# Forgetting attention and a bilinear FFN on one core: row sums of P on the tensor engine in batches 0 and 1, in a new order of work

## The chip, the cores and the metric

The program runs on one core of a Trainium2 chip. The core has a matrix engine (TensorE, here PE, with its weight loads shown apart as PEld), a vector engine (VectorE, DVE), a scalar engine (ScalarE, ACT), a general engine (GpSimd, POOL) and a queue engine (SyncE, SP) that here only issues DMAs. Data lie in SBUF, 128 partitions wide; PE writes to PSUM, eight banks of 128 x 512 fp32. The metric is the device time of one execution in microseconds. The kernel before takes 419.19 us (median of two runs, 418.51 and 419.87).

## The reference

Two stages. First attention with a forget gate, for 8 batches, 8 heads, 576 positions and a head size of 64:

```
scores = q @ k^T / 8
cum    = cumsum(log(clip(f, 1e-4, 1)))          # over positions
scores = scores + cum[query] - cum[key], and -1e9 above the diagonal
P      = exp(scores - rowmax);  P = P / sum(P)
x      = P @ v
```

Then, with x laid out as 4608 tokens of 512 numbers, `out = ((x @ w_a) * (x @ w_b)) @ w_out` with an inner width of 1536.

The term cum[query] is the same for a whole row of scores, so the softmax drops it; the kernel needs only cum[key].

## The kernel before, in words

**Tiles.** A tile t is a pair of heads of one batch: 8 batches x 4 pairs = 32 tiles, numbered 4 x batch + pair. The 576 query rows of a tile fall into blocks i = 0 to 3 of 128 rows and block 4 of 64 rows. For the blocks 0 to 3 both heads have their own rows of scores; for block 4 the two heads lie in the upper and lower 64 partitions. Scores are grouped in PSUM tiles `sc` (two buffers): group 0 holds blocks 1 and 0, then 2, 3 and 4.

**A tile's stages.** q and k are loaded (`load_qk`, from SP), cast to fp16 (`cast_qk`), transposed on PE into PSUM `psT` and copied to `qT` and `kT`. PE makes the scores (line 390). For batch 0 PE adds the decay to them, from the row `crow`, which holds cum as a high and a low fp16 part, and DVE takes the row maxima (line 474). For the other batches DVE adds the decay from `spread`, a copy of cum on all partitions, and takes the maximum in the same instruction (line 500). ACT makes P = exp (lines 527 and 531) into `PA` (blocks 0 to 2) or `PB` (blocks 3 and 4), in fp16, and with `accum_out` the row sums too, which come out by one more ACT instruction, the accumulator read. DVE takes their reciprocals (lines 539 and 541), POOL multiplies P by them (line 549). Then P is transposed: for batch 0 on PE through PSUM `psP` (line 569) and a copy, for the others by a DMA issued on SP (line 563). PE multiplies with v (`do_pv`, line 591; `do_pv4` for block 4, line 607) into the bank `pv`, which has one buffer, and DVE casts the result into x, stored transposed as `xT` (lines 217 and 618). For the batches 0 and 1 this is done in two parts, blocks 0 and 1 and blocks 2 and 3, so that the first tokens are ready early.

**FFN.** `ffn` takes 256 to 512 tokens at a time: 12 times `psa` and `psb` on PE (line 861), ACT's cast of psa to `a`, DVE's product `ht` (line 872); then `pso` (line 881), a copy to `osb` and a store. It needs the x of all four tiles of its tokens, and the weights, which POOL loads with a cast (line 365). `psa`, `psb`, `pso`, `psT`, `psP` and `scd` share three PSUM banks, `ff`.

**Start.** f is loaded four times in quarters of 32 partitions (two DMAs from ACT's queue, two from POOL's, line 173), clipped, passed through ln, summed by a scan on DVE (line 187), and made into `crow` (lines 189 and 190). SP stores cum to DRAM, from where `spread` is read.

**Order.** Every piece of work is an `Op` with its engine or engines, a planned duration, dependencies and a priority. A planner has used them once; what the program runs is its answer, written out in two strings. `ORDER` is the sequence of all ops, and `CHOICE` the engine of each op that could go to several (D, A or P). Each engine runs its instructions in this sequence. Dependencies and durations of an `Op` no longer act when the program is built; waits come from the data that the instructions read and write.

Of the kernel before, what the change touches and what calls it, by code (L numbers as in the profile page):

```python
# [9 lines left out]
FP32 = mybir.dt.float32  # L10
# [15 lines left out]
def kernel(  # L26
# [39 lines left out]
    lowrow = perm.tile([128, 1], FP32, tag="lowrow", name="lowrow")  # L66
# [3 lines left out]
    def constants():  # L70
        make_identity(nc, ident16)
        nc.gpsimd.memset(lowrow, 0.0)
        for x in pickh:
            nc.gpsimd.memset(x, 0.0)
        for m in range(4):
            x = slice(32 * m, 32 * m + 32)
            nc.gpsimd.tensor_copy(out=pick[x, :], in_=ident16[x, x])
            nc.gpsimd.tensor_copy(out=pickh[m // 2][x, :], in_=ident16[x, x])
            if m % 2:
                nc.gpsimd.memset(lowrow[x, :], -1.0)  # L80
# [12 lines left out]
    def paddings():  # L93
        for x in PB:
            nc.gpsimd.memset(x[:, 12, 64:128], 0.0)
        for i in range(2):
            nc.gpsimd.memset(nv[i][64:128, NSB - 1, :, :], 0.0)
# [11 lines left out]
            "LA0": 1, "LA1": 1, "LA2": 1, "LA3": 1, "PA": 4, "PB": 2, "PTA": 3, "PTB": 2, "st": 6, "ht": 14, "a16": 3, "osb": 2,  # L109
# [13 lines left out]
    osb_pool = pool("osb", RING["osb"])  # L123
    ps = pool("ps", 1, space=bass.MemoryType.PSUM)
# [35 lines left out]
    def f_tiles():  # L160
        x = [s_pool.tile([128, 1024], FP32, tag="S", name=n) for n in ("cum_f", "cum_l")]
        cw["f"], cw["l"] = (t[:, 0:S] for t in x)
        cw["1"], cw["h"] = (t[:, S:].bitcast(FP16)[:, 0:S] for t in x)

    def f_load(_):
        f_rows(nc.scalar, 0)

    def f_rows(eng, c):
        if not cw:
            f_tiles()  # L170
# [7 lines left out]
    o_f = Op("ACT", 2.05, f_load, prio=-310, land=0.3)  # L178
    s_users = [take(o_f, "S") for _ in range(2)]
    o_f2 = Op("POOL", 1.3, lambda _: f_rows(nc.gpsimd, 1), prio=-310, land=0.3)  # L180
    o_c = Op("POOL", 4.5, lambda _: constants(), prio=-300)
    o0 = Op("DVE", 0.3, lambda _: (nc.vector.memset(warm, 1.0), nc.vector.memset(cw["1"], 1.0)), prio=-300)
    o_w = Op("ACT", 2.2, warm_table(LN), [o0], prio=-300)
    o1 = Op("DVE", 0.45, lambda _: nc.vector.tensor_scalar(out=cw["f"], in0=cw["f"], scalar1=1e-4,
                                                           scalar2=1.0, op0=MAX, op1=MIN), [o_f, o_f2], prio=-300)
    o2 = Op("ACT", 0.7, lambda _: nc.scalar.activation(out=cw["l"], in_=cw["f"], func=LN), [o1, o_w], prio=-300)
    o3 = Op("DVE", 1.35, lambda _: nc.vector.tensor_tensor_scan(
        out=cw["f"], data0=cw["1"], data1=cw["l"], initial=0.0, op0=MUL, op1=SUB), [o2, o0], prio=-300)
    o4 = Op("DVE", 0.45, lambda _: nc.vector.tensor_copy(out=cw["h"], in_=cw["f"]), [o3], prio=-300)
    o5 = Op("DVE", 0.75, lambda _: nc.vector.scalar_tensor_tensor(  # L190
        out=crow, in0=cw["h"], scalar=lowrow[:, 0:1], in1=cw["f"], op0=MUL, op1=ADD), [o4, o_c], prio=-300)
# [4 lines left out]

    o6 = Op("SP", 1.1, cum_store, [o3], prio=-300, land=0.4)
    o_e = Op("ACT", 1.4, warm_table(EXP), [o2], prio=-300)
    for u in s_users:
        u.extend([o_f2, o0, o1, o2, o3, o4, o5, o6])  # L200
# [79 lines left out]
    PSPREAD = {t for t in range(4, 8)}  # L280
    DECP = tuple(range(1))
# [240 lines left out]
    def do_exp(t, i, h):  # L522
# [3 lines left out]
        if i == 4:  # L526
            nc.scalar.activation(out=p_blocks(t, 4), in_=T[("s" if direct else "z", t, 4)], func=EXP, bias=st[:, 8:9],  # L527
                                 scale=sign, accum_out=st[:, 18:19])
# [49 lines left out]
    def do_pv(t, rows, parts):  # L578
# [6 lines left out]
        for j in range(rows[-1] + 1):  # L585
            for i in rows:
# [7 lines left out]
                first = False  # L594

    def do_pv4(t, o=None):
# [5 lines left out]
        if own:  # L602
            o = ps.tile([128, 512], FP32, tag="pv", bufs=1, name="pv4")[:, 0:64]
        T[("pv4", t)] = o
        for j in range(NSB):
# [9 lines left out]

    def do_ev4(t):
# [5 lines left out]
    EXPD = {0: 0.39, 1: 0.505, 2: 0.61, 3: 0.72, 4: 0.775}  # L622
    NORM = {0: 0.37, 1: 0.48, 2: 0.6, 3: 0.7, 4: 0.74}
# [14 lines left out]
    def attention(t, base):  # L638
# [12 lines left out]
        if not direct:  # L651
            if t in PSPREAD:
# [3 lines left out]
                for h in range(2):  # L656
                    bm = Op("PE", 512 * COLS, lambda _, h=h: spread_mm(t, h), [o5, bc0] + bcs, prio=prio(0) - 5, mode="full", name=f"bm{t}")
# [15 lines left out]
        for gs in ([(0,), (1,), (2, 3)] if b in EARLY else [(0, 1), (2, 3)]):  # L673
            deps = [kq_ops[(w, b, pr)] for w in "qk"] + [o_c] + ([o5] if direct else bcs)
# [27 lines left out]
            for u in (kq_users[("q", b)], kq_users[("k", b)]):  # L702
                u.append(qk)
        for g, gi in [(g, groups[g]) for g in ((0, 1, 3, 2) if t in MASKP else (0, 1, 2, 3))]:
            qk, sc, su = qk_of[g], sc_of[g], None
            for i in gi:
                part = part_of(t, i)
                mxs = []
                for h in range(1 if direct else 2):
# [22 lines left out]
                    mxs.append(mx)  # L732
                es = []
                for h in range(1 if i == 4 else 2):
                    ex = Op("ACT", EXPD[i], lambda _, i=i, h=h: do_exp(t, i, h),
                            mxs if i == 4 or direct else mxs[h:h + 1], prio=prio(g),
                            name=f"exp{t}.{i}")
                    ex.tail = 0.005
# [15 lines left out]
                su.extend(es)  # L754
                rc = Op("DVE", 0.16, lambda _, i=i: do_recip(t, i), es, prio=prio(g))
# [75 lines left out]
        for rows in ([(0, 1), (2, 3)] if b in EARLY else [(0, 1, 2, 3)]):  # L831
# [3 lines left out]
            pv = Op("PE", n * 128 * COLS * 1.05, lambda _, rows=rows, parts=parts: do_pv(t, rows, parts),  # L835
# [3 lines left out]
            ev = Op("DVE", 0.15 + 0.00106 * 128 * len(rows), lambda e, rows=rows: do_ev(e, t, rows), [pv], prio=p - 1,  # L839
                    name=f"ev{t}")  # L840
# [6 lines left out]
        pv4 = Op("PE", 0.15, lambda _: do_pv4(t), [*trs["B"], *v_ops[b]], prio=p, mode="col", name=f"pv4{t}")  # L847
        pvu4 = take(pv4, "pv")
        ev4 = Op("DVE", 0.22, lambda _: do_ev4(t), [pv4], prio=p - 1)
# [110 lines left out]
    for n in cuts:  # L960
# [3 lines left out]
        0 1 3 4 19 13 25 31 2 37 20 5 21 6 14 22 7 23 15 26 12 16 260 8 24 11 17 9 54 32 27 18 261 57 28 63 33  # L964
        30 58 262 65 29 59 64 55 263 34 69-71 36 99 264 60 66 35 102 38 39 41 234 10 144 103 108 110 109 104 40
# [3 lines left out]
        56 175 138 220 75 139 81 221 176 183 184 207 87 76-78 241 228 82 229 88 83 242 101 243 118 163 80 79 164  # L969
# [8 lines left out]
        384 385 460 470 301 467 468 289 386 290 296 297 469 291 292 232 1676-1678 479 317 298 1679 374 410 411  # L978
# [132 lines left out]
```

## Time and profile before

| | |
|---|---|
| runs | 418.51 and 419.87 us, median 419.19 |
| profiled execution | 415.86 us, its span 414.1 us |
| PE, DVE, ACT, POOL busy | 391.0, 301.3, 276.9, 254.7 us |
| POOL, products of P (line 549) | 90.1 us for PA, 67.8 us for PB |
| ACT, accumulator reads of PA after scores with spread | 32.3 us, 168 of 192 ns |
| DVE, reciprocals (lines 541, 539) | 18.7 and 4.9 us, 160 in all |

The span runs from the first to the last instruction. A line of a group of instructions gives the line of the kernel, the engine, the operation, output and input, shapes and count; then the time in which at least one of them was busy and the mean duration of one in ns; then the idle time of the engine ahead of them and who ended it. Durations overlap a little: small instructions of one engine start up to 0.09 us before the end of the one ahead. A line of the chain gives start, length and what was last to end there. PE's busy time includes the modelled tails of matmuls, so a full PE is not PE at its peak.

### The profile page before, as it was taken

How to read it: one execution, taken by the hardware profiler on the slowest of the kernel's cores; microseconds unless marked ns; L12 is line 12 of the kernel's file. 1: busy time of each engine (PE TensorE's matmuls, PEld its weight loads, DVE VectorE, ACT ScalarE, POOL GpSimd, SP SyncE). 2: the span in 40 equal slices, each digit the busy share in tenths (PEclk: the TensorE clock that was granted, in tenths of full speed). 3: DMA queues.
4: the chain of work that ended last, by engine and by line, in shares of the span. 5: the costliest groups of instructions: out<-in, count | busy, mean ns of one | idle time of the engine just before them, and what ended most of it. 6: DMA issues, size and time to landing. Idle time of an engine off the chain costs nothing.

```text
span 414.1 us, 10945 instructions
## 1 busy us (share of the span) xinstructions
PE 391.0 (94%) x3860; PEld 212.0 (51%) x3860; DVE 301.3 (73%) x1002; ACT 276.9 (67%) x788; POOL 254.7 (62%) x442
## 2 busy tenths in 40 slices
PE   0688999998999999999999999999999999999996
PEld 0445785765755544444444544454444444444552
DVE  2889998996878958867987889678777885342240
ACT  2786899775867797766777687687787583231231
POOL 8699698766876867674886687676675745000000
PEclk9999999998999999999999999999999999999999
DMA  8899799999999999999979999999689727300202
GB/s 272 175 220 258 172 210 228 236 206 268 294 239 218 286 229 192 267 215 281 192 206 249 237 271 220 246 211 244 170 181 221 185 57 145 116 1 2 101 2 77
DMA packets 153528, 80.72 MB, mean 195 GB/s; under 512 B 130784, under 2 KB 133344, under 8 KB 153472
## 3 DMA queue, kind: packets, MB, share of 16 engines
q1 hardware_dynamic: 149536, 75.01, 77.1%
q0 software_dynamic: 3856, 4.87, 7.0%
q8 instruction: 30, 0.49, 0.5%
q14 instruction: 26, 0.21, 0.2%
q10 hardware_dynamic: 80, 0.15, 0.1%
HBM read 52.20 MB, written 9.58 MB: 149 GB/s over the span
## 4 chain that ended last, share of the span: by engine, by line
PE 82%; ACT 5%; DVE 4%; DMA 4%; POOL 2%; issue 1%; SPq 1%; POOLq 0%; DVEq 0%; ACTq 0%
PE psa L861 22%; PE pso L881 21%; PE psb L861 21%; PE sc L390 9%; PE pv L591 5%; ACT PA L531 2%; PE psT L258 2%; DMA wout<-in_k_dram 2%; DVE st L474 1%; DMA xT<-PA 1%; PE psP L569 1%; DVE S L500 1%; ACT PB L531 1%; PE sc L607 1%; SPq L563 1%
## 5 line engine op out<-in xcount | busy, mean ns | idle before, releaser
L500 DVE CUSTOM_DVE_ANT_0 S<-sc,spread 64x576 f32<-64x576 f32 (+4 forms) x232 | 125.3, 561 | 8.3 <-PE sc L390 3.5
L861 PE MATMUL psa<-xT,wa 128*128 128x512 f16 (+2 forms) x528 | 115.8, 342 | 0.9 <-DVE ht L872 0.5
L861 PE MATMUL psb<-xT,wb 128*128 128x512 f16 (+2 forms) x528 | 115.6, 342 | 0.3 <-ACT PTB L213 0.3
L549 POOL TENSOR_SCALAR PA<-PA,st 128x128 f16<-128x128 f16 (+2 forms) x192 | 90.1, 483 | 21.0 <-DVE st L541 13.9
L872 DVE TENSOR_TENSOR ht<-psb,a 128x512 f16<-128x512 f32 (+2 forms) x132 | 77.7, 590 | 34.8 <-PE psb L861 28.3
L213 ACT CAST a<-psa 128x512 f16<-128x512 f32 (+2 forms) x132 | 66.4, 504 | 53.4 <-PE psa L861 46.6
L881 PE MATMUL pso<-wout,ht 128*128 128x512 f16 x432 | 99.0, 382 | 0.4 <-DVE osb L217 0.4
L531 ACT ACTIVATE PA<-S,st 128x256 f16<-128x256 f32 (+2 forms) x168 | 84.2, 505 | 12.6 <-DVE st L500 12.5
L549 POOL TENSOR_SCALAR PB<-PB,st 128x512 f16<-128x512 f16 (+1 forms) x96 | 67.8, 715 | 28.1 <-DVE st L541 12.0
L861 PEld LDWEIGHTS <-wb 128*128 128x128 f16 x528 | 50.8, 98 | 40.8 <-issue 0.4
L861 PEld LDWEIGHTS <-wa 128*128 128x128 f16 x528 | 49.0, 98 | 41.3 <-issue 2.6
L881 PEld LDWEIGHTS <-ht 128*128 128x128 f16 x432 | 40.9, 98 | 47.7 <-issue 1.1
L531 ACT ACTIVATE PB<-S,st 128x512 f16<-128x512 f32 x56 | 40.2, 719 | 13.6 <-DVE st L500 12.4
L390 PE MATMUL sc<-kT,qT 64*128 64x128 f16 (+5 forms) x480 | 43.8, 278 | 3.9 <-ACT PA L531 2.2
L531 ACT ACTIVATION_READ_ACCUMULATOR PA<-S,st 128x1 f32 x168 | 32.3, 192 | 0.0
L390 PEld LDWEIGHTS <-qT 64*128 64x128 f16 (+1 forms) x480 | 17.3, 97 | 26.7 <-issue 20.8
L527 ACT ACTIVATE PB<-S,st 128x576 f16<-128x576 f32 x28 | 21.7, 776 | 12.3 <-issue 5.4
L541 DVE RECIPROCAL st<-st 128x2 f32<-128x2 f32 x128 | 18.7, 157 | 14.6 <-ACT PB L531 8.2
L217 DVE CAST xT<-pv 128x512 f16<-128x512 f32 (+1 forms) x40 | 23.0, 576 | 7.5 <-PE pv L591 7.4
L500 DVE CUSTOM_DVE_ANT_1 S<-sc,spread 128x256 f32<-128x256 f32 x48 | 19.8, 419 | 10.3 <-PE sc L607 8.2
L466 POOL TENSOR_SCALAR_AFFINE_SELECT spread<-spread 128x256 f32<-128x256 f32 x24 | 9.8, 408 | 28.0 <-DVE st L500 27.9
L459 POOL TENSOR_SCALAR_AFFINE_SELECT spread<-spread 128x768 f32<-128x768 f32 x24 | 20.9, 872 | 9.1 <-DMA spread<-cum_d 9.1
(85 smaller groups left out, 418.1 us busy)
## 6 DMA issues: line engine op xcount, KB each, us to landing
spread<-cum_d SPq DMA_DIRECT2D x24, 576.0 KB, 5.8
out_dram<-osb SPq DMA_DIRECT2D x36, 256.0 KB, 3.3
q<-in_q_dram SPq DMA_DIRECT2D x15, 576.0 KB, 5.9
k<-in_k_dram SPq DMA_DIRECT2D x15, 576.0 KB, 5.4
v<-in_v_dram SPq DMA_DIRECT2D x32, 256.0 KB, 4.5
wout<-in_moe_w_out_dram POOLq DMA_DIRECT2D x3, 512.0 KB, 6.6
v<-in_v_dram SPq DMA_DIRECT2D x8, 128.0 KB, 5.1
wa<-in_moe_w_a_dram POOLq DMA_DIRECT2D x2, 512.0 KB, 7.5
```

The costliest lines, as they stand in the source:

```text
L213: nc.scalar.copy(out=out_, in_=in_)
L217: VEC[e].tensor_copy(out=out_, in_=in_)
L390: nc.tensor.matmul(out=dst, lhsT=lhsT, rhs=rhs, start=start, stop=stop, skip_group_check=True)
L459: nc.gpsimd.affine_select(out=c[:, :, 0:SM].rearrange("p h (j k) -> p h j k", k=128), in_=c[:, :, SM:2 * SM].rearrange("p h (j k) -> p h j ...
L500: nc.vector.tensor_tensor_reduce(out=o, in0=x, in1=y, scale=-1.0, scalar=3e38, op0=ADD, op1=MIN, accum_out=m)
L527: nc.scalar.activation(out=p_blocks(t, 4), in_=T[("s" if direct else "z", t, 4)], func=EXP, bias=st[:, 8:9], scale=sign, accum_out=st[:, 1 ...
L531: nc.scalar.activation(out=p_blocks(t, i)[:, :, h, :], in_=(T[("s", t, i)][:, h, :] if direct else T[("z", t, i)][:, h * n:h * n + n]).rea ...
L549: VEC[e].tensor_scalar(out=p, in0=p, scalar1=st[:, c:c + 1], scalar2=1.0, op0=MUL, op1=MUL)
L591: nc.tensor.matmul(out=o[HP[h], 128 * i:128 * i + 128], lhsT=vt[:, j, pr + NP * h, :], rhs=pt[:, base_blk[i] + 2 * block_at(t, i, j) + h, ...
L861: nc.tensor.matmul(out=p[:, 0:n], lhsT=w16[:, db, 128 * fb:128 * fb + 128], rhs=xTflat[db][:, t0:t0 + n], start=(db == 0), stop=(db == 3))
L872: nc.vector.tensor_tensor(out=ht[:, 0:n], in0=T.pop(("psb", t0, fb))[:, 0:n], in1=T.pop(("a16", t0, fb))[:, 0:n], op=MUL)
L881: nc.tensor.matmul(out=o, lhsT=T[("ht", t0, fb)][:, 128 * tb:128 * tb + 128], rhs=wout16[:, fb, :], start=(fb == 0), stop=(fb == 11))
```

## The change

In the batches 0 and 1 (`SUMP`) P stays as the exp gives it. ACT's exps there have no `accum_out`, DVE takes no reciprocals of sums, POOL makes no products. Instead PE multiplies the same transposed P once more with a 128x64 tile of ones, right behind the product with v: each of the 64 partitions of a head then holds the row sums, in unused columns of the same bank (for blocks 0 and 1 columns 256 to 511, for 2 and 3 columns 0 to 255; for block 4 columns 64 to 127). DVE takes the reciprocal of these columns (256 or 64 wide) into a tile `rs` in SBUF (one buffer), and multiplies pv by it when it writes x, where before it cast. The transposes follow the exps directly.

The preparation of f is new as well: two loads from SP, behind the first load of q, into partitions 0 to 31 and 64 to 95; all steps on 96 partitions in two column pieces, 0 to 255 and 256 to 575; crow's high part by a copy, its low part by two subtractions of 32 partitions, one on DVE and one on POOL. The scores of the first group need only the first piece.

`ORDER` and `CHOICE` are new throughout. On the engines: PE gets 160 matmuls of 128 columns and 80 of 64 with ones. POOL loses 72 products. ACT loses 36 x 2 = 72 accumulator reads. DVE loses 40 small reciprocals, gets 16 of 128x256 and 8 of 128x64, and 24 products in place of 24 casts. Of batch 0's eight casts of q and k POOL made six and now makes one, the others are DVE's and ACT's; two copies of `spread` go from DVE to ACT, one of v from DVE to ACT. The sizes of the FFN's parts are the same.

```diff
+    ones = perm.tile([128, 64], FP16, tag="ones", name="ones")
...
+    FR = slice(0, 96)
+
+    def f_load(half):
         rows = f.rearrange("b (h p) s -> h b p s", h=2)
-        for half in range(2):
-            eng.dma_start(out=cw["f"][64 * half + 32 * c:64 * half + 32 * c + 32, :], in_=rows[half])
+        nc.sync.dma_start(out=cw["f"][64 * half:64 * half + 32, :], in_=rows[half])
...
+    def low_part(e, half, lo, hi):
+        r = slice(64 * half, 64 * half + 32)
+        VEC[e].tensor_tensor(out=crow[64 * half + 32:64 * half + 64, lo:hi], in0=cw["f"][r, lo:hi],
+                             in1=crow[r, lo:hi], op=SUB)
...
+    for lo, hi in ((0, 256), (256, S)):
+        n = hi - lo
+        o1 = Op("DVE", 0.06 + 0.00073 * n, lambda _, lo=lo, hi=hi: clip(lo, hi), [o0, *o_f], prio=-300, name="fclip")
...
+    SUMP = tuple(range(2))
...
+        sums = {} if t // NP in SUMP else {"accum_out": st[:, 10 + c:11 + c]}
         nc.scalar.activation(out=p_blocks(t, i)[:, :, h, :],
...
-                             func=EXP, scale=sign, bias=st[:, c:c + 1], accum_out=st[:, 10 + c:11 + c])
+                             func=EXP, scale=sign, bias=st[:, c:c + 1], **sums)
...
+        if b in SUMP:
+            for i in rows:
+                c = 128 * (i + 2) % 512
+                pt = T[("PT", part_of(t, i), t)]
+                for j in range(i + 1):
+                    for h in range(2):
+                        nc.tensor.matmul(out=o[HP[h], c:c + 128], lhsT=ones,
+                                         rhs=pt[:, base_blk[i] + 2 * block_at(t, i, j) + h, :], start=False,
+                                         stop=(j == i), skip_group_check=True)
...
+        if b in SUMP:
+            for j in range(NSB):
+                for h in range(2):
+                    for x, w in ((0, vt[:, j, pr + NP * h, :]), (64, ones)):
+                        nc.tensor.matmul(out=o[HP[h], x:x + 64], lhsT=w, rhs=pb[:, 8 + j, 64 * h:64 * h + 64],
+                                         start=(j == 0 and x == 0), stop=(j == NSB - 1), skip_group_check=True)
+            return
...
+    def do_rs(t, rows):
+        n = 64 if rows[0] == 4 else 128 * len(rows)
+        o = T[("pv4", t)] if rows[0] == 4 else T[("pv", t, rows)]
+        c = 64 if rows[0] == 4 else 128 * (rows[0] + 2) % 512
+        x = T[("rs", t, rows[0])] = rs_pool.tile([128, 256], FP32, tag="rs", name="rs")
+        nc.vector.reciprocal(out=x[:, 0:n], in_=o[:, c:c + n])
+
+    def do_scaled(t, rows):
+        b, pr = divmod(t, NP)
+        x = T.pop(("rs", t, rows[0]))
+        if rows[0] == 4:
+            nc.vector.tensor_tensor(out=xT[pr][:, b, SF:S], in0=T.pop(("pv4", t))[:, 0:64], in1=x[:, 0:64], op=MUL)
+            return
+        c = slice(128 * rows[0], 128 * rows[-1] + 128)
+        nc.vector.tensor_tensor(out=xT[pr][:, b, c], in0=T.pop(("pv", t, rows))[:, c], in1=x[:, 0:128 * len(rows)], op=MUL)
...
+                if b in SUMP:
+                    st_users.extend(es)
+                    norms.setdefault(part, []).extend(es)
+                    norm_of.extend((i, x) for x in es)
+                    continue
                 rc = Op("DVE", 0.16, lambda _, i=i: do_recip(t, i), es, prio=prio(g))
...
     ORDER = """
-        0 1 3 4 19 13 25 31 2 37 20 5 21 6 14 22 7 23 15 26 12 16 260 8 24 11 17 9 54 32 27 18 261 57 28 63 33
...
+        26 0 1 20 32 38 44 3 4 27 2 28 5 11 21 29 12 6 30 22 7 8 19 31 13 14 9 23 24 33 18 34 10 61 25 39 16 223
...
```

More of the change, by code (lines that the diff above doesn't have):

```diff
@@ L93, in paddings @@
     def paddings():
+        nc.gpsimd.memset(ones, 1.0)
         for x in PB:
@@ L162, in f_tiles @@
         cw["f"], cw["l"] = (t[:, 0:S] for t in x)
[L163 to L170, printed above, removed]
-        rows = f.rearrange("b (h p) s -> h b p s", h=2)
-        for half in range(2):
-            eng.dma_start(out=cw["f"][64 * half + 32 * c:64 * half + 32 * c + 32, :], in_=rows[half])
+        cw["1"] = x[0][:, S:].bitcast(FP16)[:, 0:S]
+    FR = slice(0, 96)
@@ L175, in warm_table, with f_ones @@
+    def f_load(half):
+        rows = f.rearrange("b (h p) s -> h b p s", h=2)
+        nc.sync.dma_start(out=cw["f"][64 * half:64 * half + 32, :], in_=rows[half])
+    def f_ones():
+        nc.vector.memset(warm, 1.0)
+        nc.vector.memset(cw["1"][FR, :], 1.0)
+        nc.vector.memset(cw["f"][32:64, :], 1.0)
     def warm_table(func):
         return lambda _: nc.scalar.activation(out=warm, in_=warm, func=func)
-    o_f = Op("ACT", 2.05, f_load, prio=-310, land=0.3)
-    s_users = [take(o_f, "S") for _ in range(2)]
@@ L180 @@
[L180 to L191, printed above, removed]
+    def clip(lo, hi):
+        x = cw["f"][FR, lo:hi]
+        nc.vector.tensor_scalar(out=x, in0=x, scalar1=1e-4, scalar2=1.0, op0=MAX, op1=MIN)
@@ L195, in cum_store @@
             nc.sync.dma_start(out=cum_d[:, half * S:half * S + S], in_=cw["f"][64 * half:64 * half + 32, :])
+    f_tiles()
+    o_f = [Op("SP", 0.5, lambda _, half=half: f_load(half), prio=-310, land=0.3, name=f"ldf{half}") for half in range(2)]
+    for o in o_f:
+        o.issue, o.units = 0.5, 32
+    s_users = [take(o_f[0], "S") for _ in range(2)]
+    o_c = Op("POOL", 4.5, lambda _: constants(), prio=-300)
+    o0 = Op("DVE", 0.3, lambda _: f_ones(), prio=-300)
+    o_w = Op("ACT", 2.2, warm_table(LN), [o0], prio=-300)
+    crow_ops, lns = [], []
+    o3 = None
+    for lo, hi in ((0, 256), (256, S)):
+        n = hi - lo
+        o1 = Op("DVE", 0.06 + 0.00073 * n, lambda _, lo=lo, hi=hi: clip(lo, hi), [o0, *o_f], prio=-300, name="fclip")
+        o2 = Op("ACT", 0.2 + 0.00083 * n, lambda _, lo=lo, hi=hi: nc.scalar.activation(
+            out=cw["l"][FR, lo:hi], in_=cw["f"][FR, lo:hi], func=LN), [o1, o_w], prio=-300, name="fln")
+        o3 = Op("DVE", 0.02 + 0.00232 * n, lambda _, lo=lo, hi=hi: scan(lo, hi), [o2, o0] + ([o3] if lo else []),
+                prio=-300, name="fscan")
+        o4 = Op("DVE", 0.06 + 0.0007 * n, lambda _, lo=lo, hi=hi: nc.vector.tensor_copy(
+            out=crow[FR, lo:hi], in_=cw["f"][FR, lo:hi]), [o3], prio=-300, name="fhi")
+        o5 = [Op(None, {"DVE": 0.06 + 0.0013 * n, "POOL": 0.15 + 0.0013 * n},
+                 lambda e, half=half, lo=lo, hi=hi: low_part(e, half, lo, hi), [o4], prio=-300, name=f"flo{half}") for half in range(2)]
+        crow_ops.append(o5)
+        lns.append(o2)
+        for u in s_users:
+            u.extend([o0, o1, o2, o3, o4, *o5])
     o6 = Op("SP", 1.1, cum_store, [o3], prio=-300, land=0.4)
-    o_e = Op("ACT", 1.4, warm_table(EXP), [o2], prio=-300)
+    o_e = Op("ACT", 1.4, warm_table(EXP), lns, prio=-300)
     for u in s_users:
-        u.extend([o_f2, o0, o1, o2, o3, o4, o5, o6])
+        u.extend([o_f[1], o6])
     o_p = Op("POOL", 4.0, lambda _: paddings(), [o_c], prio=-100)
@@ L838, in attention @@
             pvu = take(pv, "pv")
-            ev = Op("DVE", 0.15 + 0.00106 * 128 * len(rows), lambda e, rows=rows: do_ev(e, t, rows), [pv], prio=p - 1,
-                    name=f"ev{t}")
+            if sums:
+                rs = Op("DVE", 0.06 + 0.00106 * 128 * len(rows), lambda _, rows=rows: do_rs(t, rows), [pv], prio=p - 1,
+                        name=f"rs{t}")
+                rsu = take(rs, "rs")
+                pvu.append(rs)
+            ev = Op("DVE", 0.15 + 0.00106 * 128 * len(rows),
+                    lambda e, rows=rows, sums=sums: do_scaled(t, rows) if sums else do_ev(e, t, rows), [pv, *([rs] if sums else [])],
+                    prio=p - 1, name=f"ev{t}")
+            if sums:
+                rsu.append(ev)
             pvu.append(ev)
```

160 lines of the change are left out of this document (82 added, 78 removed), and 77 rows, old and new, of the table ORDER.

## The prediction

> **What bounds the kernel now.** I read the page's busy times first, then the busy time by stage, then the chain that ended last, then the rows by form.
>
> ```profile
> PE 391.0 (94%) x3860; PEld 212.0 (51%) x3860; DVE 301.3 (73%) x1002; ACT 276.9 (67%) x788; POOL 254.7 (62%) x442
> 14.80:39.10 24.30, 20.66 (x266) 12.72 (x267) 21.52 (x47) 18.24 (x61) 19.83 (x39) 1.00 0.99 220
> 39.10:52.00 12.90, 12.06 (x199) 8.96 (x197) 12.12 (x36) 11.37 (x35) 9.20 (x13) 1.00 0.88 174
> 52.00:93.30 41.30, 41.22 (x552) 28.23 (x552) 38.40 (x151) 35.60 (x110) 33.56 (x54) 1.00 1.10 221
> 93.30:100.10 6.80, 4.95 (x34) 2.37 (x28) 3.33 (x15) 3.31 (x13) 4.41 (x9) 0.75 1.12 273
> ```
>
> PE fills 94% of the span, but the shares by stage (window; then PE, PEld, DVE, ACT, POOL, granted clock, DMA, GB/s) say more. From 14.8 us (first row maximum) to 39.1 us (just after the first FFN matmul starts) DVE is the fullest, 21.5 of 24.3 us. From 39.1 to 52 PE, DVE and ACT are all at 88% or more. From 52 on PE is at 99.8%. Everything after 110 us is a PE stream that the change leaves alone, so a microsecond won or lost before it moves the end by the same. Before the first FFN matmul the chain passes from engine to engine, and one stall lies at 93 us:
>
> ```profile
> 1.83 7.41 DMA wout<-in_k_dram
> 11.76 0.97 POOL k L217
> 12.73 1.29 DVE crow L190
> 14.07 0.72 PE sc L390 x12
> ...
> 90.69 4.71 DMA xT<-PA
> ```
>
> The first scores wait for crow, which is late because f lands late, at 8.8 us. At 93.3 us PE waits 1.85 us for a transpose by DMA, then runs at half clock for 3.4 us (mean 0.75 in that stage): 2.0 + 1.7 = 3.7 us lost.
>
> **The change, part by part.**
>
> *Start.* f comes by SP behind q, half as many bytes, and the decay is made in two column pieces; batch 0's q and k casts leave POOL for DVE and ACT. DVE's list from the old rows: q lands at 0.81 + 4.0 = 4.8 us; cast 0.83 (row of the 128x512 k cast); f soon after, say 6.0; the clips 0.40 + 0.46 (0.73 us for 576 columns); k landed at 7.2 us and has two small loads more ahead of it on SP but less f traffic beside it, so about the same; casts 0.83 + 0.9 to 8.9; scans and copies 0.60 + 0.29 + 0.76 + 0.33 to 10.9; low part, kT and second low part 0.42 + 0.75 + 0.49 to 12.5. The first maximum then stands at about 12.5 instead of 14.8 us: **-2.3 us**. Bounds: -0.5 (only ACT's 2.0 us and POOL's 1.35 us of f issues gone, k as late as now) to -3.5 (k cast as soon as f is clipped). The memsets (0.54 us) lie in the wait for q. POOL issues its weight loads (0.66 to 0.80 us each) with fewer products ahead of them; no FFN matmul waits for a weight load now, so I count nothing. The new dependencies of the first exps are the planner's alone; the order that it gave is written out.
>
> *Up to the first FFN matmul.* DVE is the bound, so I count its instructions from the first maximum to the write of the fourth x. Gone: 13 reciprocals at the 0.07 us at which they follow each other, kT and qT (0.75 each), two spread copies (0.68 each), one v cast (0.69), four xT casts (0.41): 6.1 us. New: one q cast (0.85), one psP copy (0.55), four 256-wide reciprocals at 0.41 and four products at 0.42: 4.7 us. **-1.4 us**. Bounds 0 and -5.5: 27 accumulator reads of 0.205 us leave ACT in this stage. POOL's products (19.8 us busy here) mostly go too, but the chain has none of them, so I give nothing for them; each transpose is ready about 0.6 us earlier, which DVE hides.
>
> *The wide reciprocal has no row.* Nearest rows, by form and by line:
>
> ```profile
> L217 DVE CAST xT<-pv 128x256 f16<-128x256 f32 x16 | 6.6, 413 | 2.2 <-PE pv L591 2.2
> L872 DVE TENSOR_TENSOR ht<-psb,a 128x256 f16<-128x256 f32 x36 | 15.0, 418 | 2.8 <-PE psb L861 1.3 <-ACT a L213 1.1
> L541 DVE RECIPROCAL st<-st x128: 134/158/168, 18.4 to 347.8; 128x2 f32<-128x2 f32 x128
> L539 DVE RECIPROCAL st<-st x32: 134/157/166, 37.0 to 346.7; 128x1 f32<-128x1 f32 x32
> ```
>
> A cast from PSUM takes 413 ns for 256 columns and 684 for 512: 1.06 ns a column over 0.14 us. A reciprocal of two elements has the median of one element plus 1 ns. That is one column a step, so I take 0.41 us, and 0.22 us for 64 columns (217 ns, the 64-wide cast). Lower end: 0.28 us, two columns a step, as the 128x576 cast within SBUF has it (459 ns); upper end: the second element may hide up to 10 ns inside the scatter (158 to 168), so 0.15 + 256 x 0.010 = 2.7 us. The Trainium skill (VectorE: DVE Perf Modes, section "First, the fixed hardware budget") speaks against the change here: reciprocal is an iterative divide with a repeat count of 8. By it, if each element holds the engine for eight steps, my estimate would be 0.14 + 8 x 0.27 = 2.3 us; the trace's 1 ns from one element to two does not agree, though no run here shows a wide one.
>
> *PE's sums.* 160 matmuls of 128 columns and 80 of 64, all with ones as the weights. In the timeline pairs follow each other at 0.055 us:
>
> ```profile
> 88.00 0.22 PE L591 MATMUL pv<-xT,nv 128*64 128x128 f16 x2
> 88.06 0.22 PE L591 MATMUL pv<-PTB,nv 128*64 128x128 f16 x2
> 88.11 0.22 PE L591 MATMUL pv<-xT,nv 128*64 128x128 f16 x2
> ```
>
> 80 pairs x 0.055 = 4.4, and 40 pairs of 64 at 0.031 = 1.2: 5.6 us at least. Whole bursts with their tails (14 in 0.51, 10 in 0.28) give 160 x 0.036 + 80 x 0.028 = 8.0 at most. They join bursts that exist, so I take 6.0. The 24 before the first FFN matmul (0.8 us) lie under DVE's bound: **+5.2 us**.
>
> *The pv bank* (one buffer) is held for a reciprocal and a product instead of one cast: 0.41 us longer, 24 times. The DVE instruction that waits for pv has the next maxima behind it, as the cast had; on PE the next pv waits. The new order has scores, FFN or transposes between two pv nearly everywhere, so I take +0.5 us; bounds 0 and 24 x 0.41 = 10, reached only with nothing between.
>
> *From 39 to 110 us.* ACT loses 45 more accumulator reads (8.6 us) and POOL about 45 products. Only from 38.5 to 51.8 does ACT stand densely on the chain, with 12 reads, 2.9 us, there; by 52 PE's own queue takes over. **-1.0 us**, bounds 0 and -2.9. DVE gets 12 wide and 8 narrow reciprocals, 6.7 us, loses 26 small ones (1.9 to 4.2) and some copies (1.6): +0.9 to +3.2 us in stages where it is at 93 to 94%. PE's sums stretch the same stages, so most of this hides beside them; 0, upper end +3.
>
> *Clock.* The profile prints full clock at the start, yet the same six transposes took 0.85 us at 24 us and 0.51 at 33:
>
> ```profile
> 24.17 0.85 PE L569 MATMUL psP<-ident,PA 128*128 128x128 f16 x6
> 32.77 0.51 PE L569 MATMUL psP<-ident,PA 128*128 128x128 f16 x6
> ```
>
> So PE is at half rate until about 32 us. I leave that as it is, since DVE sets the pace there. The stall at 93 us I leave too: its place hangs on the new order of SP's transposes, and 3.7 us goes into the range both ways.
>
> Sum: -2.3 - 1.4 + 5.2 + 0.5 - 1.0 = **+1.0 us**: a span of 415.1, and 416.9 for the profiled execution (415.86 now, 1.8 of it outside the span). The runs shown have a median of 419.19, 3.3 above the profiled one; on that scale the forecast is **420 us**, no change. A measurement of this kernel tells about 2% (8.4 us) from no change.
>
> **Rivals.**
>
> *A. The wide reciprocal takes several steps an element.* For it: the upper end above. Against: one and two elements cost the same. At 2.7 us it adds 16 x 2.3 + 8 x 0.57 = 41 us to DVE before about 110 us, where DVE has some 12 us free (2.8 + 0.8 + 2.9 + 3.5 + about 2). It decides as soon as the added time passes those 12 us, at about 1.1 us a piece. 41 - 12 = +29 us on the forecast: some 449 us, slower. Chance 0.18. The eight steps of the Trainium skill (VectorE: DVE Perf Modes) would make it, as an estimate, 34 - 12 = +22 us, 442.
>
> *B. The relief is worth more than DVE's count.* Start -3.5, the stage to FFN -5.5, ACT -2.9, no stall at 93 us -3.7, sums 5.6 - 0.8 = +4.8: -10.8 us, 408 us. For it: ACT and POOL lie next to DVE in the chain before 39 us, and both are unloaded. Against: DVE's 21.5 of 24.3 us. Chance 0.16.
>
> *C. The gain is not spent, or the order brings its own stall.* The transposes still wait for DMA (share above 1.0 from 52 to 100 us): sums +6, bank +1, one more stall like that at 93 us +3.7, start -2.3: +8.4, 428 us, at the 2% mark. Chance 0.18. That the change frees POOL without any use for it is part of this case.
>
> The forecast, 411 to 425, has 0.48. The range **406 to 435** takes in B's mean, C and a mild A, and leaves about 0.2 out, mostly A. Faster by over 2%: B mostly, 0.17; slower: A and a third of C and a little more, 0.26; within 2%: 0.57.
>
> **What would show it.** The 128x256 reciprocal's mean (0.41 or over 2 us); the first maximum at 12 to 13 us; the first FFN matmul at 34 to 36 us instead of 38.7; no accumulator reads from ACT in the first two batches; PE's ones matmuls summing to 6 us; a stage 52 to 93 us in which PE stays above 99%. DVE at 98% there with PE waiting for xT would mean A. A PE wait of 2 us or more for a transpose, with the clock row below 9, would mean C.

## The result and the profile after

The changed kernel takes 434.54 us (median; 433.36 and 435.72), 1.037 times the kernel before (95% interval 1.032 to 1.043): slower by about 15.4 us. The profiled execution took 433.36 us with a span of 431.7 (before 415.86 and 414.1). The time lies inside the forecast's range, 406 to 435, but at its end, and the likeliest case, 420 us and no change, is not what happened.

The busy times of the changed kernel, as on its page (engine, busy us, share of the span, instructions), and the chain that ended last by engine and by line:

```profile
PE 397.2 (92%) x4100; PEld 217.9 (50%) x4100; DVE 327.2 (76%) x988; ACT 277.1 (64%) x725; POOL 211.8 (49%) x363
...
PE 74%; DVE 17%; DMA 3%; issue 3%; ACT 1%; SPq 0%; POOL 0%; DVEq 0%; ACTq 0%
PE psa L948 20%; PE psb L948 19%; PE pso L968 19%; PE sc L414 7%; DVE rs L663 6%; PE pv L617 5%; DVE S L524 4%; PE psT L281 2%; DMA PTA<-PA 2%; DVE st L498 2%; DVE ht L959 1%; DMA k<-in_k_dram 1%; DVE xT L672 1%; PE psP L595 1%; PE sc L649 1%
```

POOL lost 43 us of work as the change says. DVE, which was to end up about even, gained 26. The instruction at line 663, the wide reciprocal, holds 6% of the chain. The same stages as before (window; its length, then busy us of PE, PEld, DVE, ACT, POOL, granted clock, DMA share, GB/s):

```profile
14.80:39.10 24.30, 17.25 (x241) 11.44 (x240) 21.44 (x29) 17.07 (x37) 10.17 (x15) 0.93 1.16 236
39.10:52.00 12.90, 11.39 (x193) 8.59 (x194) 12.13 (x28) 8.03 (x15) 2.58 (x4) 1.00 1.27 206
52.00:93.30 41.30, 35.19 (x574) 24.52 (x570) 40.01 (x102) 28.44 (x60) 9.01 (x10) 1.00 0.77 165
93.30:100.10 6.80, 5.71 (x60) 4.24 (x61) 6.70 (x17) 3.64 (x8) 0.00 (x0) 1.00 1.09 244
```

From 52 to 93 us PE was full before, 41.22 of 41.3 us. Now it is busy for 35.2 us, and DVE for 40.0, 97%. ACT and POOL have more idle time than ever and nothing to fill it with. The rows by form show what fills DVE (busy us, mean ns; then its idle time ahead of them):

```profile
L663 DVE RECIPROCAL rs<-pv 128x256 f32<-128x256 f32 x16 | 28.0, 1752 | 1.4 <-PE pv L627 1.3
L672 DVE TENSOR_TENSOR xT<-pv,rs 128x256 f16<-128x256 f32 x16 | 6.8, 422 | 0.4
L663 DVE RECIPROCAL rs<-pv 128x64 f32<-128x64 f32 x8 | 4.4, 552 | 0.1
L669 DVE TENSOR_TENSOR xT<-pv,rs 128x64 f16<-128x64 f32 x8 | 1.8, 221 | 0.2
```

The products cost what the forecast gave them. The reciprocal of 256 columns takes 1.75 us, not 0.41, and that of 64 columns 0.55, not 0.22: (1752 - 552) / 192 = 6.25 ns a column over 0.15 us, where a column of a cast takes 1.06. The excess is 16 x 1.34 + 8 x 0.33 = 24.1 us of DVE.

### The profile page after: what moved, and what is told of

Read it like the earlier page. It is cut to its first block, busy times and chain, and to the rows that moved or that the text cites. A ratio compares the mean times of both kernels' runs of the same rounds, so it can differ in the third digit from the quotient of the medians.

```text
span 431.7 us, 11273 instructions
## 1 busy us (share of the span) xinstructions
PE 397.2 (92%) x4100; PEld 217.9 (50%) x4100; DVE 327.2 (76%) x988; ACT 277.1 (64%) x725; POOL 211.8 (49%) x363
## 4 chain that ended last, share of the span: by engine, by line
PE 74%; DVE 17%; DMA 3%; issue 3%; ACT 1%; SPq 0%; POOL 0%; DVEq 0%; ACTq 0%
PE psa L948 20%; PE psb L948 19%; PE pso L968 19%; PE sc L414 7%; DVE rs L663 6%; PE pv L617 5%; DVE S L524 4%; PE psT L281 2%; DMA PTA<-PA 2%; DVE st L498 2%; DVE ht L959 1%; DMA k<-in_k_dram 1%; DVE xT L672 1%; PE psP L595 1%; PE sc L649 1%
## 5 line engine op out<-in xcount | busy, mean ns | idle before, releaser
L948 PE MATMUL psb<-xT,wb 128*128 128x512 f16 (+2 forms) x528 | 115.2, 341 | 1.1 <-ACT a L236 0.8
L575 POOL TENSOR_SCALAR PA<-PA,st 128x384 f16<-128x384 f16 (+2 forms) x144 | 67.1, 478 | 20.8 <-DVE st L567 16.1
L575 POOL TENSOR_SCALAR PB<-PB,st 128x512 f16<-128x512 f16 (+1 forms) x72 | 50.4, 709 | 14.2 <-DVE st L567 6.2
L557 ACT ACTIVATE PB<-S,st 128x512 f16<-128x512 f32 x56 | 40.1, 718 | 13.3 <-DVE st L524 11.4
L414 PE MATMUL sc<-kT,qT 64*128 64x256 f16 (+5 forms) x480 | 43.4, 276 | 5.2 <-ACT PA L557 3.1
L663 DVE RECIPROCAL rs<-pv 128x256 f32<-128x256 f32 (+1 forms) x24 | 32.5, 1352 | 1.4 <-PE pv L627 1.3
L552 ACT ACTIVATE PB<-S,st 128x576 f16<-128x576 f32 x28 | 21.7, 777 | 10.9 <-issue 4.8
L236 ACT COPY osb<-pso 128x512 f32<-128x512 f32 x19 | 10.9, 575 | 25.6 <-PE pso L968 13.4
L617 PEld LDWEIGHTS <-nv 128*64 128x64 f16 x640 | 19.3, 110 | 15.9 <-issue 8.4
L557 ACT ACTIVATION_READ_ACCUMULATOR PA<-S,st 128x1 f32 x144 | 27.3, 189 | 0.0
```

The costliest lines, as they stand in the source:

```text
L236: nc.scalar.copy(out=out_, in_=in_)
L414: nc.tensor.matmul(out=dst, lhsT=lhsT, rhs=rhs, start=start, stop=stop, skip_group_check=True)
L557: nc.scalar.activation(out=p_blocks(t, i)[:, :, h, :], in_=(T[("s", t, i)][:, h, :] if direct else T[("z", t, i)][:, h * n:h * n + n]).rea ...
L575: VEC[e].tensor_scalar(out=p, in0=p, scalar1=st[:, c:c + 1], scalar2=1.0, op0=MUL, op1=MUL)
L617: nc.tensor.matmul(out=o[HP[h], 128 * i:128 * i + 128], lhsT=vt[:, j, pr + NP * h, :], rhs=pt[:, base_blk[i] + 2 * block_at(t, i, j) + h, ...
L663: nc.vector.reciprocal(out=x[:, 0:n], in_=o[:, c:c + n])
```

## The experiments

### What a reciprocal costs by itself

A small kernel of such instructions (and, behind them, copies, ACT's ln and exp and POOL's power), four of each width, first out of SBUF (line 40, shown here), then seven of these widths out of PSUM (line 43):

```
for n in (1, 2, 4, 8, 16, 32, 64, 128, 256, 512):
    for _ in range(4):
        nc.vector.reciprocal(out=dst[:, 0:n], in_=src[:, 0:n])
```

> A small kernel that leaves out all of the reference's work and writes a constant. It runs DVE's reciprocal four times at each of several widths, 1 to 512 columns, out of SBUF and out of PSUM, then copies of the same widths, ACT's ln and exp, and POOL's power. Theory: a reciprocal costs 0.15 us plus 6.25 ns a column, whatever memory it reads: 512 columns 3.35 us, 256 columns 1.75, 64 columns 0.55, 16 columns 0.25, and the first columns lie hidden, since one and two elements take 156 and 158 ns in the kernel. Rival: the 1.75 us in the changed kernel come from the PSUM bank or from crowding, and out of SBUF in an idle kernel 256 columns take 0.4 to 0.5 us.

Rows by form of the small kernel:

```profile
L43 DVE RECIPROCAL dst<-p 128x512 f32<-128x512 f32 x4 | 13.4, 3357 | 0.1
L43 DVE RECIPROCAL dst<-p 128x256 f32<-128x256 f32 x4 | 7.0, 1757 | 0.1
L40 DVE RECIPROCAL dst<-src 128x256 f32<-128x256 f32 x4 | 7.0, 1753 | 0.1
...
L40 DVE RECIPROCAL dst<-src 128x16 f32<-128x16 f32 x4 | 1.0, 253 | 0.1
...
L40 DVE RECIPROCAL dst<-src 128x4 f32<-128x4 f32 x4 | 0.7, 178 | 0.1
L43 DVE RECIPROCAL dst<-p 128x2 f32<-128x2 f32 x4 | 0.7, 170 | 0.1
L43 DVE RECIPROCAL dst<-p 128x1 f32<-128x1 f32 x4 | 0.7, 168 | 0.2
L40 DVE RECIPROCAL dst<-src 128x2 f32<-128x2 f32 x4 | 0.7, 166 | 0.1
L40 DVE RECIPROCAL dst<-src 128x1 f32<-128x1 f32 x4 | 0.6, 149 | 0.1
```

The price goes with the instruction. For 256 columns it is the same to 5 ns out of SBUF and PSUM, in an idle kernel and in a crowded one (1753, 1757 and 1752 ns). Out of SBUF the widths follow 0.153 us + 6.25 ns a column, from 2 columns up. The rival, 0.4 to 0.5 us for 256 columns out of SBUF, is refuted by 1753 ns. One column alone lies off the line: the second adds 17 ns out of SBUF (149 to 166) and 2 out of PSUM (168 to 170). So the expectation that the first columns lie hidden does not hold out of SBUF, where the kernel's small reciprocals read too.

### The reciprocal's price taken away

```diff
-        nc.vector.reciprocal(out=x[:, 0:n], in_=o[:, c:c + n])
+        nc.vector.tensor_copy(out=x[:, 0:n], in_=o[:, c:c + n])
```

> The changed kernel with the wide reciprocal replaced by a DVE copy of the same columns of the pv bank; the division is left out, x comes out as the product with the sums. Everything else stays, waits and order too. A copy of 256 columns takes 0.41 us (the row of the cast), so DVE does 16 x 1.34 + 8 x 0.33 = 24 us less. Theory (the reciprocal's price is the whole loss): the time falls by 24 us less what DVE has free, 12 to 24 us, to 411 to 422 us, the forecast of 420 included; PE above 95% from 52 to 93 us. Rival (the new order, the pv bank or PE's sums lose the time): 428 us or more.

417.14 us, 0.997 times the kernel before (0.993 to 1.001). So everything in the change but the reciprocal's extra time, new order and PE's sums included, comes out about even, and the 24 us of DVE cost 434.54 - 417.14 = 17.4 us (16.8 if each is taken against the kernel before that ran beside it, 419.19 and 418.60). The stages of this kernel:

```profile
14.80:39.10 24.30, 19.74 (x296) 13.83 (x296) 21.27 (x38) 20.14 (x44) 9.19 (x14) 1.00 1.11 240
39.10:52.00 12.90, 12.80 (x244) 10.21 (x246) 11.86 (x32) 10.50 (x21) 4.41 (x5) 1.00 1.07 183
52.00:93.30 41.30, 40.83 (x652) 28.23 (x647) 38.84 (x144) 33.17 (x79) 12.54 (x17) 1.00 1.15 239
93.30:100.10 6.80, 6.79 (x79) 4.14 (x77) 5.46 (x19) 3.96 (x15) 3.36 (x6) 1.00 1.17 214
```

PE is back at 99% from 39 us on, and the stall that stood at 93 us before is gone. The first FFN matmul starts at 34.2 us, as forecast (34 to 36), where the changed kernel has it at 38.2 and the kernel before at 38.7.

### PE's sums taken away

In the first kernel the matmuls with ones are left out and the reciprocal reads other columns; in the second the copy stands in place of the reciprocal as well.

```diff
-        if b in SUMP:
-            for i in rows:
...
-                        nc.tensor.matmul(out=o[HP[h], c:c + 128], lhsT=ones,
...
-                    for x, w in ((0, vt[:, j, pr + NP * h, :]), (64, ones)):
+                    for x, w in ((0, vt[:, j, pr + NP * h, :]),):
```

> The changed kernel without the matmuls with ones; the reciprocal stays as wide and reads the product's own columns instead, so the row sums are left out. Theory (DVE's reciprocals set the pace in the first 110 us): PE's time there is covered, 430 to 434.5 us. Rival (PE's sums are what costs): 427 us or less.

> Both edits: no matmuls with ones, and copies in place of the reciprocals; row sums and division are left out. Theory: once DVE is relieved PE sets the pace again and its sums come out at the price of the forecast, so this is 4 to 6 us below the run with copies alone. Rival (PE is not the bound in the new order): within 2 us of the run with copies alone.

Without sums but with reciprocals: 433.05 us, 1.036 (1.033 to 1.039), against 434.54 with them: DVE covers PE's sums, as expected. Without both: 416.22 us, 0.995 (0.992 to 0.997), only 0.9 us below the copies alone, not the 4 to 6 expected, and the two intervals overlap. The rival has the number here, and the trace says where the gain went. A window of the kernel without both, and PE's longest wait of it:

```profile
80.00:93.30 13.30, 10.71 (x100) 7.39 (x99) 10.59 (x41) 8.69 (x25) 2.97 (x5) 0.87 1.13 227
```

```profile
PE pv L635 <- DMA PTB<-PB: 2.5, 1, 2.5
```

With the sums PE was busy for 13.20 of these 13.3 us. Without them it arrives early, stands 2.5 us for a transpose by DMA and then, by an estimate from the granted clock of 0.87, loses 0.13 x 13.3 = 1.7 us: 4.2 of the 5.2 us that the sums were to cost. It is a stall like that of the kernel before (1.8 us, mean clock 0.75), at another transpose.

### The new start alone

The kernel before with the new preparation of f, its place on SP and the new engines for batch 0's casts; the rest of the order kept, and `SUMP` empty. From the edit of the kernel before:

```diff
-    o_f = Op("ACT", 2.05, f_load, prio=-310, land=0.3)
...
+    o_f = [Op("SP", 0.5, lambda _, half=half: f_load(half), prio=-310, land=0.3, name=f"ldf{half}") for half in range(2)]
...
+    SUMP = ()
```

> The kernel before with one part of the change alone: the new preparation of f, its place in SP's queue and the new engines for batch 0's casts of q and k; row sums, products of P and the rest of the order as before. The whole computation is done. Theory (forecast): the first row maximum comes about 2 us earlier and the end with it, a ratio of 0.995 to 0.997 to the kernel before. Rival (the gain is lost before the first FFN matmul, where other work sets the pace): 0.999 to 1.003.

419.34 us against 419.18, 0.9995 (0.997 to 1.002): nothing that can be measured arrives at the end, as the rival has it. The first row maximum (timeline of this kernel) starts at 13.42 instead of 14.82 us. Of these 1.4 us 0.6 are left at the first FFN matmul, 38.1 instead of 38.7, and 0.6 us lies inside the interval:

```profile
13.42 0.69 DVE L498 TENSOR_REDUCE st<-sc 128x2 f32<-128x512 f32 x1
```

```profile
PE pv L617 <- DMA xT<-PA: 2.0, 2, 1.9
PE pv L617 <- DMA PTB<-PB: 0.9, 1, 0.9
PE pv L617 <- DMA PTA<-PA: 0.4, 1, 0.4
```

The second fence is PE's waits from 80 to 112 us (total us, times, longest): 3.3 us for transposes by DMA, where the kernel before has one of 1.8 and then, as the prediction estimates, loses 1.7 us more to the clock. Here the granted clock from 93.3 to 100.1 us is 1.00, so the two stalls come out alike. Which of them takes the last 0.6 us, if it is lost, the traces do not show.

### More of the same

```diff
         nc.vector.reciprocal(out=x[:, 0:n], in_=o[:, c:c + n])
+        nc.vector.reciprocal(out=x[:, 0:n], in_=o[:, c:c + n])
```

> The changed kernel with each wide reciprocal done twice; the result is the same. DVE gets 32.4 us more before 136 us. Theory (the free time of DVE is used up by the first 24 us): nearly all of it shows, 460 to 467 us. Rival (some 12 us or more of each addition find cover beside PE and the DMAs): 455 us or less.

470.36 us, somewhat above the expected 460 to 467: 35.8 us more for 32.4 us of DVE. The first 24 us cost 0.72 us each, the next 32 cost 1.1: no cover is left. The granted clock of PE is 0.57 from 39.1 to 52 us, where the changed kernel has 1.00; that may be the 3.4 us beyond DVE's own time, but no run shows it alone:

```profile
39.10:52.00 12.90, 10.73 (x105) 7.23 (x105) 10.85 (x16) 5.70 (x10) 4.39 (x5) 0.57 0.90 153
```

### DVE's time, or the bank that it holds

In the changed kernel PE stands 10.2 us before `pv` until the product `xT` frees the single bank, and 0.7 us before `psa` for x itself; with the copies it stands 1.2 in all. That could be the cause, or only the place where a late DVE is seen. PE's waits for `xT` in the changed kernel, 14 to 130 us, all five lines:

```profile
PE pv L617 <- DVE xT L672: 6.5, 4, 2.1
...
PE pv L644 <- DVE xT L672: 2.6, 3, 1.3
...
PE pv L617 <- DVE xT L669: 0.8, 2, 0.5
...
PE psa L948 <- DVE xT L672: 0.7, 2, 0.4
...
PE pv L644 <- DVE xT L669: 0.3, 1, 0.3
```

So here DVE keeps the work but does it on a tile of its own, behind the product that frees the bank:

```diff
-        nc.vector.reciprocal(out=x[:, 0:n], in_=o[:, c:c + n])
+        nc.vector.tensor_copy(out=x[:, 0:n], in_=o[:, c:c + n])
...
         nc.vector.tensor_tensor(out=xT[pr][:, b, c], in0=T.pop(("pv", t, rows))[:, c], in1=x[:, 0:128 * len(rows)], op=MUL)
+        for n in (64, 64, 28):
+            nc.vector.reciprocal(out=aside[:, 0:n], in_=aside[:, 0:n])
```

> As the run with copies (division left out), but DVE does the reciprocals' extra work on a small tile of its own, right after the product that frees the pv bank: three reciprocals of 64, 64 and 28 columns behind a wide piece, one of 28 behind a narrow one, 16 x 1.36 + 8 x 0.33 = 24 us. So DVE has as much to do before 130 us as in the changed kernel, but the pv bank and x are free 1.34 us earlier, 16 times. Theory (DVE's time itself is the loss): 430 to 436 us, like the changed kernel. Rival (the hold of the single pv bank, and with it PE's wait for the next product, is the loss): 417 to 424 us. In between, the two shares can be read off.

434.12 us, 1.035 (1.030 to 1.039): the time of the changed kernel, to 0.4 us. PE's waits for `xT` are down to 2.4 us, and the time has not moved. So DVE's time is the loss, and the wait for the bank was its symptom. Where the lateness goes instead, ACT's waits show: its exps need DVE's row maxima (`st`), and from 14 to 130 us they stand for them 28.2 us in the changed kernel, 12.4 with the copies and 27.3 with the reciprocals aside (6.5 in the kernel before). The line for `PA` behind scores with spread, in these three:

```profile
ACT PA L557 <- DVE st L524: 10.6, 11, 2.9
```

```profile
ACT PA L557 <- DVE st L524: 3.4, 7, 1.5
```

```profile
ACT PA L559 <- DVE st L526: 12.1, 10, 2.6
```

The stretch from 39.1 to 130 us in four kernels, before, after, with copies, and with the reciprocals aside:

```profile
39.10:130.00 90.90, 88.04 (x1181) 59.84 (x1178) 77.75 (x290) 73.69 (x225) 69.96 (x111) 0.98 1.09 227
```

```profile
39.10:130.00 90.90, 77.83 (x1198) 54.75 (x1198) 86.84 (x232) 59.09 (x140) 28.49 (x41) 1.00 0.87 174
```

```profile
39.10:130.00 90.90, 90.28 (x1368) 62.72 (x1369) 82.00 (x288) 70.29 (x178) 43.49 (x65) 1.00 1.08 225
```

```profile
39.10:130.00 90.90, 80.49 (x1206) 56.25 (x1205) 85.78 (x276) 59.40 (x141) 30.33 (x42) 0.98 0.90 175
```

DVE is busy for 86.8 and 85.8 of 90.9 us in the two slow ones, and PE is busy 12.5 and 9.8 us less than with the copies. With the copies DVE had 8.9 us idle here, and the full reciprocals could use 4.8 of them.

### 1/sum on ACT

ACT has idle time, so 1/sum can be exp(-ln(sum)) there. Three kernels compute the whole reference in this way: all 24 pieces on ACT; only the eight wide pieces of blocks 2 and 3; and all on ACT with each product two DVE instructions later.

```diff
-        nc.vector.reciprocal(out=x[:, 0:n], in_=o[:, c:c + n])
+        nc.scalar.activation(out=x[:, 0:n], in_=o[:, c:c + n], func=LN)
+        nc.scalar.activation(out=x[:, 0:n], in_=x[:, 0:n], func=EXP, scale=-1.0)
...
+        nc.scalar.preload_act_table_set("natural_log_exp_and_others")
```

The last line loads one table for both functions before the first instruction of ACT; all the kernels with ln on ACT from here on have it.

> The changed kernel with 1/sum made on ACT as exp(-ln(sum)), two instructions, 0.80 us for 256 columns and 0.48 us for 64 by the small kernel's rows; the whole computation is done. ACT's table for both functions is loaded once, so the second load (1.28 us) goes. DVE loses 32.4 us, ACT gets 16 x 0.80 + 8 x 0.48 = 16.6 us. In the run with copies ACT has 4.2, 2.4 and 8.1 us free in the stages 14.8 to 39.1, 39.1 to 52 and 52 to 93.3 us, and 5.4 from there to 110. Theory (only DVE's time was the loss, and ACT's free time takes the work): 414 to 421 us, like the run with copies. Rival (ACT, which makes every exp that PE waits for, becomes the bound): 425 us or more.

> As the run before it, but only the eight wide pieces of blocks 2 and 3 go to ACT; the eight of blocks 0 and 1 and the eight narrow ones stay DVE reciprocals. The whole computation is done. DVE loses 14.0 us against the changed kernel, ACT gets 6.4. Theory (DVE's time counts at about 0.7 of its length, 17.4 of 24 us in the run with copies): 434.5 - 0.7 x 14 = 424 to 426 us, more than with ACT alone. Rival (ACT is as tight as DVE, so sharing is best): at or below the run with ACT alone.

> The kernel with 1/sum on ACT, in another order: each product of pv and 1/sum is put behind the next two DVE instructions, as long as no later pv and no reader of x comes between. The whole computation is done. In the run with ACT alone DVE, though relieved of 32 us, stood still 21.7 us before its products, since ACT reaches the ln behind exps that are ahead of it in its queue. Theory (DVE's standstill, not its busy time, is the loss; the order was written for a reciprocal of 0.33 us): most of the 21.7 us go and the time falls from 432.6 to 420 to 426 us. Rival (the hold of the single pv bank through two more instructions on another engine is the loss, whoever waits): 429 us or more, since the bank is then held longer still.

432.59 us (1.033; 1.029 to 1.037), 433.29 (1.032; 1.029 to 1.036) and 433.06 (1.035; 1.030 to 1.039). None of the three differs from another by more than its interval, none is a repair, and in all three the rival's number came out (in the second within the noise). In the first, DVE is relieved of 32 us and does not run ahead. DVE's wait for 1/sum, first with all on ACT (two lines), then in the later order:

```profile
DVE xT L673 <- ACT rs L664: 18.0, 11, 3.3
DVE xT L670 <- ACT rs L664: 3.7, 5, 1.5
```

```profile
DVE xT L673 <- ACT rs L664: 6.9, 8, 1.4
```

The later order took two thirds of the wait for 1/sum away, 21.7 to 6.9 us, and the time did not follow. But DVE's standstill only moved: from 14.8 to 130 us DVE is busy for 81.3 of 115.2 us in both kernels, and in the later order it stands 9.1 us for `psb` instead of 2.1. PE's waits for `xT` grew from 8.2 to 13.5 us, as the rival, the longer hold of the bank, has it. So this run does not tell DVE's standstill from the hold of the bank. Another candidate is ACT's time, put aside in the same way as DVE's:

```diff
+        nc.vector.tensor_copy(out=x[:, 0:n], in_=o[:, c:c + n])
+        for _ in range(2 if n > 64 else 1):
+            nc.scalar.activation(out=aside, in_=aside, func=LN)
+            nc.scalar.activation(out=aside, in_=aside, func=EXP, scale=-1.0)
```

> The changed kernel with a copy in place of the reciprocal (division left out), and ACT doing the ln and exp work at the same places in its queue on a small tile of its own, which waits for nothing and for which nobody waits: four instructions of 64 columns for a wide piece, two for a narrow one, 0.24 us each, 19.2 us in all. One table load as in the run with ACT alone. Theory (ACT's time is not what loses the time in the run with ACT alone, the waits are): 417 to 421 us. Rival (ACT's time delays the exps and is the loss): 427 us or more.

422.85 us, 1.011 (1.007 to 1.015), between the two expectations. The ln and exp put aside took 20.6 us of ACT by the trace (19.2 were planned) and cost 5.7 us over the copies. With all 24 pieces on ACT they take 16.7 us, so at most about a third of the 15.4 us by which that version lies above the copies is ACT's time. The other 10 us or so are left for the waits in line, pv to ACT to DVE to the bank, which the runs do not divide further.

The last try frees the bank early: DVE casts the product into x at once, and POOL multiplies x by 1/sum in SBUF.

```diff
+            do_ev("DVE", t, rows)
...
+        nc.gpsimd.tensor_tensor(out=xT[pr][:, b, c], in0=xT[pr][:, b, c], in1=x[:, 0:n], op=MUL)
```

> The kernel with 1/sum on ACT, and the pv bank freed early: DVE casts the product into x at once, beside ACT's ln, and POOL, which is idle here, multiplies x by 1/sum in SBUF later. The whole computation is done. The bank is held some 0.45 us as in the kernel before; no instruction of DVE waits for ACT. POOL gets 24 products. Theory (the run with ACT alone loses 5.7 us to ACT's time, as measured aside, and the rest, some 10 us, to the hold of the bank and to DVE's wait): 420 to 425 us. Rival (x is late in any case, since ln, exp and product stand one behind the other before the FFN, and POOL's and ACT's queues add to it): 429 us or more.

447.26 us, 1.066 (1.063 to 1.070), worse than the other versions with ln on ACT. The bank was not freed early, so the edit did not do what it was meant to: the cast, which reads the same PSUM tile, waited for ACT's ln in 16 of 24 pieces, and POOL then stood for the cast, with its own casts of q, k and v queued behind. DVE's wait, then POOL's, 14 to 130 us:

```profile
DVE xT L240 <- ACT rs L663: 18.2, 11, 2.9
DVE xT L667 <- ACT rs L663: 9.8, 5, 7.3
```

```profile
POOL xT L676 <- DVE xT L240: 42.2, 11, 9.8
POOL xT L676 <- ACT rs L664: 11.5, 5, 5.3
```

Why the cast waited for another reader no run shows, and what an early release would bring is still open. No version that computes the whole reference beat the kernel before. The run with copies, an estimate of what this order could reach with a division that costs no more than a copy, is 0.3% below it, and its interval takes in no change at all.

## Why the prediction was wrong in its likeliest case

**The step that failed** is "The wide reciprocal has no row": "That is one column a step, so I take 0.41 us". Rival A is what happened, in a milder size: 1.75 us, between the 0.41 taken and the 2.7 of the upper end. The reading behind it was that a second element costs 1 ns: medians of 157 and 158 ns, in rows whose single instructions run from 134 to 168 ns. A column costs 6.25 ns, and a difference of that size is lost in such a spread. Alone and out of SBUF the second column adds 17 ns and each further one 6.25; why the two medians of the crowded kernel lie so close is not shown. Two sizes one column apart gave no slope; the upper end, which allowed for the spread, should have had more weight than 0.18. The Trainium skill (VectorE: DVE Perf Modes, section "First, the fixed hardware budget") gave the iterative divide a repeat count of 8, from which the forecast made an estimate of 2.3 us. The trace agrees that an element takes several steps: 6.25 ns a column is 5.9 times the 1.06 ns of a cast, so the estimate was too long by almost a third, but much nearer than the value taken.

**The price of rival A.** With the measured size its own sum gives 24.1 - 12 = +12 us on the forecast, 432 us; measured were 17.4 us over the copies. The 12 us called free were idle time, and only 6.6 were usable: what DVE does in a stage also waits for PE and ACT, and it stays idle in part when more is put on it (4.1 of 90.9 us from 39 to 130 us in the changed kernel). By this reading the point of decision, 1.1 us a piece, was too high too; no run has a reciprocal between 0.4 and 1.75 us.

**The rest of the sum** was +1.0 us on the span. The kernel with the copies tests it: a span of 414.0 against 414.1, a ratio of 0.997, that is -1.4 us (-3.0 to +0.2). The sum holds to 2.4 us, and neither B's 408 nor C's 428 came; but its parts do not all hold, so some of the agreement is luck:
- *Start*, -2.3 us at the first maximum: 12.92 instead of 14.82, -1.9. In the kernel with the start alone it is -1.4, of which 0.6 us are left at the first FFN matmul and nothing measurable at the end.
- *Up to the first FFN matmul*, -1.4 after the start: with the copies 34.2 us, 4.5 earlier in all, more than the forecast's 3.7. In the changed kernel four reciprocals with 5.4 us of excess lie ahead of that matmul and eat 4.0 of it (38.2 us).
- *PE's sums*, +5.2: the matmuls do fill that much of PE (110.0 us busy with them and 104.8 without, from 14.8 to 130 us, both with copies), but taken away they bring 0.9 us, since PE then stands for a transpose. The term was right for a PE that is the bound and wrong for one that is early.
- *The pv bank*, +0.5: with the copies PE waits 1.2 us for `xT`.
- *The stall at 93 us*, left at nothing with 3.7 us both ways: it goes with the copies, and comes back at 80 to 93 us without the sums.
- *ACT's reads*: 72 are gone (24 tiles x 9 = 216 are left), but no run takes them alone, so their -1.0 is not shown.

**The signs named ahead** did their work: the reciprocal's mean, and DVE at 97% from 52 to 93 us with PE at 85%, told A apart at once. The first maximum came at 12.9 us, in time; the first FFN matmul, at 38.2, did not. The wait of PE for xT was there too, but the run with the reciprocals aside shows it to be a symptom.

## What to carry to other kernels

Price an instruction that has never run at its size by its slope, and take a slope only from sizes so far apart that the spread of the rows cannot hide it; where only tiny ones are at hand, enter the operation at its upper end, or replace it by a form that stays tiny. Work that is moved onto a nearly full engine is paid there: here 24 us more on DVE, at 93% busy, came out at 0.72 us each, and the next 32 at 1.1. A wait that the profile names tells where lateness is seen; to learn whether a buffer or the engine's time causes it, keep the time and free the buffer.

## What was not expected of the hardware

- The reciprocal on DVE takes 6.25 ns a column, six times a cast's, from SBUF and from PSUM alike. One and two columns differ by 2 ns out of PSUM (168 and 170) and by 17 out of SBUF (149 and 166), so neither pair shows the slope.
- In the small kernel ACT makes 1/sum of 256 columns in 0.38 + 0.42 = 0.80 us, under half of DVE's 1.75. With the joint table set loaded by name ahead of them, both functions needed one table load (1.28 us) where the changed kernel has two; the Trainium skill (ScalarE: Activation LUTs, section "🔬 Table sets: the hidden batching unit") lists a set that holds exp and ln, and the trace agrees. The small kernel, which does not name the set, has four loads of 1.28 us for its two turns of ln and exp.
- There a power on POOL takes 41.2 us for 256 columns and 10.5 for 64, some 160 ns a column; POOL is no place for a reciprocal of this width.
